# The order of input loads in a fused state-space and bilinear feed-forward kernel: three queues for one block, and both halves of the output weights in one place

## The chip, the cores and the metric

The kernel runs on one core of a Trainium2 chip. The metric is the device time of one execution in microseconds. The core has five engines that each work through their own list of instructions: PE (TensorE, matrix products), DVE (VectorE), ACT (ScalarE), POOL (GpSimd) and SP (SyncE, which here only issues transfers). Transfers between the main memory and the core's SBUF are issued from SP, ACT or POOL; each of the three has its own queue, in which requests stand in the order of the program. In the profile's list of DMA queues q1 is SP's, q10 is ACT's and q0 is POOL's.

## The reference: what is computed

Inputs are x (4 batches, 8 heads, 768 tokens, 32 values), a decay a for each token, B and C (16 values for each token), and three weight matrices. For each batch and head a state of 16 x 32 runs through the tokens; in closed form, with cum the cumulative sum of log a,

```
y[i] = sum over j <= i of (C[i] . B[j]) * exp(cum[i] - cum[j]) * x[j]
X    = y, heads side by side: 3072 tokens x 256
out  = ((X @ w_a) * (X @ w_b)) @ w_out        # 256 -> 1536 -> 256
```

The reference takes chunks of 32 tokens and carries the state from chunk to chunk; any other chunk gives the same sums.

## The kernel before

The 768 tokens are cut into six blocks of 128. A pair is two batches' share of a block, or, in the blocks after the first, four heads of all batches where B and C are concerned: pairs 0 and 1 belong to block 0, pairs 2 and 3 to block 1, pairs 4 and 5 to block 2, and so on. For each pair `scores` (line 398) multiplies C with B, `mask` (442) applies the causal mask, `outputs` (532) multiplies with x, adds the part that comes from the state and makes the sums for the next state. The feed-forward part of block k (`unit`, `bunit`: a product with w_a, a product with w_b, a copy on ACT, a multiplication on DVE; then `out_mm` or `bout` with w_out) is woven between the scores of the later blocks, so that PE always has work.

The order is written out by hand, line by line, from line 774 on: every engine takes its instructions in the order in which the program names them, and the framework adds the waits that the data need. The PSUM banks of the feed-forward part are dealt out in advance: `bank` (129) takes the next digit of the string `BANKS`, one of four banks.

What the change touches, in the order of the program:

- Loads on SP: `load_q(nc.sync, 1)` (815) loads block 1's C and B, four batches each, 64 KB a request. Then come x for pairs 2 and 3 (`load_x32`, 721; four requests of 128 KB), B for pairs 2 and 3 (`load2(nc.sync, p, 0)`, 820; `load2` makes two requests of 64 KB here), and six of the eight requests of block 2 (846). `ALL_Q` (158) lists them: C of batches 0 to 3, then B of batches 0 to 3. The last two B requests are made on POOL (904). Behind them on SP stand `loads_b(4, 5)` (847) and the later blocks' loads.
- Weights on POOL: `load_w` (182) for w_a and w_b in halves, then `load_wo(0)` (866) and `load_wo(1)` (869) for the halves of w_out, rows 0 to 5 and 6 to 11 of the tile `Wo`. The first half is used first by `out_mm(0, 0, o[0], range(6))` (907), the second by the loop of line 930.
- Decay factors: `mid_rows` (286, tile Ps), `turned_rows` (296, tile Pt, a transpose on DVE), `batch_factors` (301, tile FC, one copy for each batch, on POOL for block 1 and on ACT for the others), `batch_inverse` (308, tile FB).
- Planes: `scale_q` (341) multiplies C with FC and B with FB into a tile `planes` on POOL; `turn` (353) transposes it on DVE into `turned`, which the scores read. `scale_bc` (324) makes bm from bn, that is B by token, for the state sums (`ds_mm`, 495).
- Masks: `mask(..., by_pool=True)` copies the scores on ACT into tmp and multiplies on POOL; otherwise DVE does it.

Of the kernel before, what the change touches and what calls it, by code (L numbers as in the profile page):

```python
# [19 lines left out]
SS = 64.0  # L20

BANKS = (
    "012313213212301230123012302103120312301230132013210320132012301230132103210321023013201320"
    "1321023102310231021302130213021302130213021302310231023102310231023102310231023102310"
)


# [1 line left out]
def kernel(  # L29
# [13 lines left out]
    nc = tc.nc  # L43

    nb, H, S, D = x.shape
# [14 lines left out]
    NT = NBLK - PJ // NBP  # L60
# [79 lines left out]
    def by_token(t_):  # L140
        return t_.rearrange("p h r n -> p (h r n)").rearrange("p (t h n) -> p t h n", t=2, h=H)

    def load1(eng, p, which, bt, i0=0, n=64, to=None):
        blk, bp = divmod(p, NBP)
        if p >= P2:
            return eng.dma_start(
                by_token(pair_in[p][which])[:, bt],
                (B, C, x)[which][2 * bp + bt, :, blk * Q : (blk + 1) * Q, :].rearrange("h q n -> q h n"),
            )
        src = (B, C, x)[which][2 * bp + bt, :, blk * Q + 2 * i0 : blk * Q + 2 * i0 + 2 * n, :]  # L150
        if to is None:
            to = pair_in[p][which]
        return eng.dma_start(  # L153
            to[64 * bt + i0 : 64 * bt + i0 + n].rearrange("i h r n -> i h (r n)"),
            src.rearrange("h (i r) n -> i h (r n)", r=2),
        )

    ALL_Q = tuple((w, b) for w in (1, 0) for b in range(nb))

    def load_q(eng, blk, parts=ALL_Q):  # L160
        if blk not in by_batch:
            by_batch[blk] = [inq.tile([128, H, 4, N], f32, name=n_, tag=n_) for n_ in ("bq", "cq")]
        return [
            eng.dma_start(  # L164
                by_batch[blk][w][32 * b : 32 * b + 32].rearrange("i h s n -> i h (s n)"),
                (B, C)[w][b, :, blk * Q : (blk + 1) * Q, :].rearrange("h (i s) n -> i h (s n)", s=4),
            )
            for w, b in parts
        ]

    def load2(eng, p, which):
        if p < P2:
            return [load1(eng, p, which, bt) for bt in range(2)]
        blk, bp = divmod(p, NBP)
        src = (B, C, x)[which][2 * bp : 2 * bp + 2, :, blk * Q : (blk + 1) * Q, :]
        return [
            eng.dma_start(  # L177
                by_token(pair_in[p][which]).rearrange("p t h n -> p (t h) n"), src.rearrange("t h q n -> q (t h) n")
            )
        ]  # L180
# [6 lines left out]
    def load_wo(half):  # L187
        return nc.gpsimd.dma_start(
            Wo[:, 6 * half : 6 * half + 6].rearrange("p (g kk) e -> p g (kk e)", kk=3),
            moe_w_out.rearrange("(g p kk) e -> p g (kk e)", p=128, kk=3)[:, 2 * half : 2 * half + 2],  # L190
        )
# [94 lines left out]
    def mid_rows(lo, hi, eng):  # L286
        k = slice(lo + NBLK - NT, hi + NBLK - NT)
        eng.tensor_tensor(
            out=Ps[:, lo:hi], in0=Pr[:, k], in1=rmid[:, k].unsqueeze(2).broadcast_to((BH, hi - lo, Q)), op=ALU.mult
        )  # L290
# [10 lines left out]
    def batch_factors(lo, hi, *bs, eng=None):  # L301
        for b in bs:
            (eng.tensor_copy if eng else nc.scalar.copy)(
                FC[32 * b : 32 * b + 32, lo:hi].rearrange("p k s h -> p (k s) h"),
                Pt[:, lo:hi].rearrange("p k s (b h) -> p (k s) b h", b=nb)[:, :, b],
            )
# [91 lines left out]
    def scores(p):  # L398
        s = st[p] if p < PJ else st["U", p]
        BT, CT = s["BT"], s["CT"]  # L400
        s["T1"] = mid.tile([128, 4, 4, Q], f16, name="t1", tag="t1")

        def score(o_, b_, c_, at):
            nc.tensor.matmul(o_, b_, c_, start=True, stop=True, skip_group_check=True, tile_position=at)  # L404

        if p >= P2:
            for j, b in itertools.product(range(4), range(nb)):
                rows = slice(32 * b, 32 * b + 32)
                score(SC[b][:, j * Q : j * Q + Q], BT[rows, j], CT[rows, j // 2], (32 * b, 0))
            return  # L410
        for e, r, m, bt in itertools.product(range(2), range(2), range(4), range(2)):
            c0 = (e * 2 + r) * Q
            o_ = SC[m][64 * bt : 64 * bt + 64, c0 : c0 + Q]
            if p >= PJ:
                bp, g = divmod(m, 2)
                row = 32 * (2 * bp + bt)
                rows = slice(row, row + 32)
                b_ = BT[rows, 2 * g + e].rearrange("p (i r) -> p r i", r=2)[:, r]
                score(o_, b_, CT[rows, g], (row, 64 * bt))
            else:  # L420
                rows = slice(32 * m, 32 * m + 32)
                score(o_, BT[rows, e, r, bt], CT[rows, bt], (32 * m, 64 * bt))
# [151 lines left out]
    def state_spread(blk):  # L574
        Sbd = mid.tile([128, H // 2, 2 * D], f16, name="spair", tag="spair")
        nc.gpsimd.tensor_tensor(
            out=Sbd.rearrange("p g (e d) -> p (g e) d", e=2),
            in0=V32[:, blk].rearrange("p g (e d) -> p (g e) d", e=2),
            in1=Ge[:, blk].unsqueeze(2).broadcast_to((128, H, D)),
            op=ALU.mult,  # L580
        )
        st["S", blk + 1] = Sbd
# [10 lines left out]
    def unit_mm(p, k2, W):  # L593
        ps = bank("aps" if W is Wa else "bps")
        for kk in range(2):
            k = 2 * k2 + kk
            for f in range(2):
                nc.tensor.matmul(  # L598
                    ps[:, kk * 2 * Q : (kk + 1) * 2 * Q],
                    W[k // 6][:, f, k % 6 // 3 * 384 : (k % 6 // 3 + 1) * 384].rearrange("p (c kk) -> p kk c", kk=3)[  # L600
                        :, k % 3
                    ],
                    X2T[:, p, :, f],
                    start=(f == 0),
                    stop=(f == 1),
                    skip_group_check=True,
                )
        return ps

    def evac_a(a_ps, on_dve=False):  # L610
        asb = ffh.tile([128, 512], f32, name="asb", tag="asb")
        (nc.vector.tensor_copy if on_dve else nc.scalar.copy)(asb, a_ps)  # L612
        return asb

    def times(p, k2, b_ps, asb, by_pool=False):
        s = st[p]
        if "hk" not in s:
            s["hk"] = ffh.tile([128, NK, 2 * Q], f16, name="hk", tag="hk")
        eng = nc.vector
        if by_pool:  # L620
            eng, b_ps = nc.gpsimd, evac_a(b_ps)
        eng.tensor_tensor(  # L622
            out=s["hk"][:, 2 * k2 : 2 * k2 + 2, :].rearrange("p k q -> p (k q)"), in0=b_ps, in1=asb, op=ALU.mult
        )

    def unit(p, k2, between=None, by_pool=False):
        a_ps = unit_mm(p, k2, Wa)
        if between:
            between()
        b_ps = unit_mm(p, k2, Wb)  # L630
        asb = evac_a(a_ps)
        return lambda: times(p, k2, b_ps, asb, by_pool)
# [78 lines left out]
    def loads_b(*ps):  # L711
        for p in ps:
            if p < NP:
                tiles(p)
                load2(nc.sync, p, 0)
# [30 lines left out]
    def spread(blk):  # L746
        if blk < NBLK - 1:
            state_spread(blk)
            state_decay(blk)
# [67 lines left out]
    for p in (2, 3):  # L817
        tiles(p)
    x_in = [load_x32(p) for p in (2, 3)]
    for p in (2, 3):  # L820
        load2(nc.sync, p, 0)
    warmup(tcp, 512, 512)
    transposes(1, apart=True)
    aps = [unit_mm(0, 0, Wa)]
# [18 lines left out]
    for m in range(3):  # L843
        mask(product(1, m))
    bps = [unit_mm(0, k2, Wb) for k2 in range(3)]
    load_q(nc.sync, 2, ALL_Q[:6])
    loads_b(4, 5)
    times(0, 0, bps[0], asb[0])
    times(0, 1, bps[1], asb[1], by_pool=True)
# [13 lines left out]
    nc.vector.reciprocal(flat(fB, 1, 2), fps[:, 2 * NBP * H : 4 * NBP * H])  # L863
    times(0, 2, bps[2], asb[2])
    turned_rows(0, 1)
    load_wo(0)
    batch_factors(0, 1, *range(nb), eng=nc.gpsimd)
    mid_rows(1, NT, nc.gpsimd)
    load_wo(1)
    go((1, 0))  # L870
    batch_inverse(0, 1)
# [12 lines left out]
        op=ALU.mult,  # L884
    )
    spread(0)
    late = ((0, 3), (0, 4), (1, 3))
    aps = [unit_mm(p, k2, Wa) for p, k2 in late]
    asb = [evac_a(a_ps) for a_ps in aps]
    batch_factors(2, NT, *range(nb))  # L890
    for (p, k2), a_sb_ in zip(late, asb):
        times(p, k2, unit_mm(p, k2, Wb), a_sb_)
        if k2 == 4:
            turn(2)
    go((0, 5))
    h = unit(1, 4)
    scores(2)
    turn(3)
    mask(product(2, 3), by_pool=True)
# [1 line left out]
    h()  # L901
    h5 = unit(1, 5)
    mask(product(2, 2), by_pool=True)
    load_q(nc.gpsimd, 2, ALL_Q[6:])
    mask(product(2, 1))
    o = [bank("ops"), bank("ops")]
    out_mm(0, 0, o[0], range(6))
    out_mm(0, 1, o[1], range(6))
    batch_factors(1, 2, 0, 1)
    h5()  # L910
    o.append(bank("ops"))
    out_mm(1, 0, o[2], range(6))
    scores(3)
    mask(product(3, 3), by_pool=True)
    batch_factors(1, 2, 2, 3)
    scale_bc(2, 0, nc.gpsimd)
    scale_bc(3, 0, nc.gpsimd)
    nc.gpsimd.memset(causal_q, SS)
# [11 lines left out]
    for c in range(3):  # L930
        p, bt = divmod(c, NBP)
# [136 lines left out]
```

## Time and profile before

| what | us |
|---|---|
| median of 3 runs | 122.37 (122.28 to 123.07) |
| the profiled execution | 122.9 |
| its span, first to last instruction | 121.2 |
| PE busy in it | 115.9 |
| DVE, ACT, POOL busy | 90.2, 67.4, 58.7 |

The profile shows one execution. A timeline line gives the start, the duration, the engine, the line of the kernel and the operation with what it writes and reads, then, in brackets, the idle time of the engine ahead of it and what ended it. Lines that say "x4" merge instructions that follow each other. An issue of a transfer has a duration of its own, the time that it held the issuing queue; from the issue to the landing of the data is a time of its own again, and is given in the list of issues. The granted clock of PE was 1.00 in every stretch that is looked at here. A list of DMA queues gives packets, megabytes and the time of the packets as a share of 16 engines; it can exceed 100% where packets overlap.

### The profile page before, as it was taken

The numbers are of one execution on the slowest core, as the hardware profiler recorded it, in microseconds if no ns is written. First come the engines' busy times: TensorE is split into PE (matmuls) and PEld (weight loads), VectorE is DVE, ScalarE is ACT, GpSimd is POOL, SyncE is SP. The second block draws the span as 40 slices with busy tenths as digits, with TensorE's granted clock in tenths as the row PEclk, the third lists the DMA queues.
The fourth block names the chain that finished last, engine by engine and source line by source line (L and its number), as shares of the span: only waits on it lengthen the run. The fifth ranks groups of instructions, "written<-read, shape, count | busy, mean of one in ns | idle before, by whom it ended". The sixth has DMA issues, their size and how long they took to land.

```text
span 121.2 us, 3577 instructions
## 1 busy us (share of the span) xinstructions
PE 115.9 (96%) x1399; PEld 75.5 (62%) x1400; DVE 90.2 (74%) x165; ACT 67.4 (56%) x135; POOL 58.7 (48%) x92
## 2 busy tenths in 40 slices
PE   7989999999999999999999999999999999999990
PEld 5646799788644478644475464775465684645880
DVE  4998889799989995599966999677899426748000
ACT  0446659648567655577566737635735637475230
POOL 7994887997479999386902994200000000000000
PEclk9999999999999999999999999999999999999999
DMA  2999999986769996999992919012001111010131
GB/s 62 135 172 194 205 216 187 206 123 135 113 90 102 145 112 119 102 108 145 200 239 89 86 5 124 7 46 92 0 0 46 44 43 48 0 43 0 49 121 52
DMA packets 59297, 12.13 MB, mean 100 GB/s; under 512 B 54480, under 2 KB 59216, under 8 KB 59280
## 3 DMA queue, kind: packets, MB, share of 16 engines
q0 software_dynamic: 20320, 3.80, 38.3%
q1 hardware_dynamic: 36432, 7.74, 33.8%
q10 hardware_dynamic: 2528, 0.36, 1.8%
q8 instruction: 11, 0.18, 0.7%
q14 instruction: 6, 0.05, 0.1%
HBM read 12.42 MB, written 3.15 MB: 128 GB/s over the span
## 4 chain that ended last, share of the span: by engine, by line
PE 68%; DMA 14%; SPq 10%; POOL 3%; issue 1%; DVE 0%; ACT 0%; POOLq 0%
PE ops L693 22%; PE aps L667 20%; PE bps L667 20%; SPq L153 8%; DMA cq<-in_C_dram 6%; DMA Wa<-in_moe_w_a_dram 5%; DMA bq<-in_B_dram 3%; PE SC L404 2%; SPq L164 2%; PE SC L473 2%; POOL xn L153 1%; PE SC L536 1%; POOL causal L225 1%; POOL planes L346 1%; DVE turned L359 0%
## 5 line engine op out<-in xcount | busy, mean ns | idle before, releaser
L612 ACT COPY asb<-aps 128x512 f32<-128x512 f32 x72 | 41.9, 586 | 15.6 <-PE aps L667 13.3
L679 DVE TENSOR_TENSOR hkb<-bps,asb 128x512 f16<-128x512 f32 x60 | 40.3, 687 | 11.9 <-ACT asb L612 10.5
L667 PE MATMUL aps<-XB,Wa 128*128 128x512 f16 x120 | 35.8, 379 | 0.0
L667 PE MATMUL bps<-XB,Wb 128*128 128x512 f16 x120 | 35.7, 379 | 0.0
L693 PE MATMUL ops<-Wo,hkb 128*128 128x256 f16 (+1 forms) x252 | 28.1, 268 | 0.0
L693 PEld LDWEIGHTS <-hkb 128*128 128x128 f16 x252 | 23.0, 98 | 3.8
L667 PEld LDWEIGHTS <-Wb 128*128 128x128 f16 x120 | 12.4, 103 | 13.5
L667 PEld LDWEIGHTS <-Wa 128*128 128x128 f16 x120 | 12.1, 103 | 11.5 <-issue 0.2
L449 DVE TENSOR_TENSOR t<-SC,causal_q 128x512 f16<-128x512 f32 x27 | 17.3, 682 | 2.4 <-PE SC L404 2.4
L705 ACT ACTIVATE osb<-ops 128x256 f32<-128x256 f32 (+1 forms) x20 | 7.6, 378 | 18.4 <-PE ops L693 18.4
L447 POOL TENSOR_TENSOR t<-tmp,causal_q 128x512 f16<-128x512 f32 x5 | 5.8, 1157 | 8.8 <-ACT tmp L446 8.8
L177 POOL DMA_DIRECT2D xn<-in_x_dram x8 | 9.5, 1190 | 0.0
L346 POOL TENSOR_TENSOR planes<-bq,FB 128x256 f16<-128x256 f32 x10 | 7.5, 770 | 2.0 <-DMA bq<-in_B_dram 1.4
L446 ACT COPY tmp<-SC 128x512 f32<-128x512 f32 x10 | 5.9, 588 | 4.1 <-PE SC L404 3.8
L346 POOL TENSOR_TENSOR planes<-cq,FC 128x256 f16<-128x256 f32 x10 | 7.6, 775 | 0.9 <-DMA cq<-in_C_dram 0.8
L449 DVE TENSOR_TENSOR t<-SC,causal 128x512 f16<-128x512 f32 x11 | 7.0, 681 | 0.7 <-PE SC L404 0.6
L622 DVE TENSOR_TENSOR hk<-bps,asb 128x512 f16<-128x512 f32 x11 | 7.2, 670 | 0.2 <-ACT asb L612 0.2
L598 PE MATMUL aps<-X2T,Wa 128*128 128x256 f16 x48 | 6.8, 274 | 0.0
L558 ACT ACTIVATE XB<-SC 128x512 f16<-128x512 f32 (+1 forms) x9 | 4.6, 548 | 4.1 <-PE SC L501 2.4
L598 PE MATMUL bps<-X2T,Wb 128*128 128x256 f16 x48 | 6.6, 273 | 0.1
L359 DVE STREAM_TRANSPOSE turned<-planes 128x384 f32<-128x384 f32 x10 | 5.5, 564 | 1.1 <-POOL planes L346 1.1
L447 POOL TENSOR_TENSOR t<-tmp,causal 128x512 f16<-128x512 f32 x5 | 5.7, 1154 | 0.3
(101 smaller groups left out, 110.6 us busy)
## 6 DMA issues: line engine op xcount, KB each, us to landing
out_dram<-osb SPq DMA_DIRECT2D x23, 128.0 KB, 1.9
cq<-in_C_dram SPq DMA_DIRECT2D x20, 64.0 KB, 2.7
bq<-in_B_dram SPq DMA_DIRECT2D x18, 64.0 KB, 3.8
bn<-in_B_dram SPq DMA_DIRECT2D x8, 128.0 KB, 3.9
xn<-in_x_dram POOLq DMA_DIRECT2D x8, 128.0 KB, 5.2
Wa<-in_moe_w_a_dram POOLq DMA_DIRECT2D x2, 384.0 KB, 7.4
Wb<-in_moe_w_b_dram POOLq DMA_DIRECT2D x2, 384.0 KB, 8.0
Wo<-in_moe_w_out_dram POOLq DMA_DIRECT2D x2, 384.0 KB, 6.8
```

The source lines that it names most:

```text
L153: return eng.dma_start(to[64 * bt + i0 : 64 * bt + i0 + n].rearrange("i h r n -> i h (r n)"), src.rearrange("h (i r) n -> i h (r n)", r=2),)
L177: eng.dma_start(by_token(pair_in[p][which]).rearrange("p t h n -> p (t h) n"), src.rearrange("t h q n -> q (t h) n"))
L346: eng.tensor_tensor(out=plane[:, c0 : c0 + 4 * step].rearrange("p (j c) s -> p j s c", c=step)[:, :, :, 0:N], in0=by_batch[blk][which][:, ...
L447: nc.gpsimd.tensor_tensor(out=o_, in0=tmp, in1=c_, op=ALU.mult)
L449: nc.vector.tensor_tensor(out=o_, in0=i_, in1=c_, op=ALU.mult)
L598: nc.tensor.matmul(ps[:, kk * 2 * Q : (kk + 1) * 2 * Q], W[k // 6][:, f, k % 6 // 3 * 384 : (k % 6 // 3 + 1) * 384].rearrange("p (c kk) -> ...
L612: (nc.vector.tensor_copy if on_dve else nc.scalar.copy)(asb, a_ps)
L622: eng.tensor_tensor(out=s["hk"][:, 2 * k2 : 2 * k2 + 2, :].rearrange("p k q -> p (k q)"), in0=b_ps, in1=asb, op=ALU.mult)
L667: nc.tensor.matmul(t_, W[k // 6][:, f, k % 6 // 3 * 384 : (k % 6 // 3 + 1) * 384].rearrange("p (c kk) -> p kk c", kk=3)[:, k % 3], XB[:, b ...
L679: return lambda: nc.vector.tensor_tensor(out=s["hk"][:, k], in0=ps[1], in1=asb, op=ALU.mult)
L693: nc.tensor.matmul(o_ps[:, 0:w], hk[:, k, c * Q : (c + 1) * Q], Wo[:, k, cs], start=(k == 0), stop=(k == NK - 1), skip_group_check=True,)
L705: nc.scalar.activation(out=o_sb[:, 0:w], in_=o_ps[:, 0:w], func=AF.Copy, scale=1.0 / (YS * YS))
```

## The change

Four loads change their queue or their place, six copies of factors change their place on ACT, and the string of banks is replaced.

- The two requests for pair 3's B go from SP to POOL, behind `spread(0)`.
- Of block 2's eight requests SP makes five (C of batch 3, B of batches 0 to 3), and ACT makes the first three (C of batches 0 to 2), at the place where POOL made two.
- `load_wo(0)` goes from ahead of `batch_factors(0, 1, ...)` on POOL to behind `mid_rows(1, NT, ...)`, directly ahead of `load_wo(1)`.
- The factors of block 2 (`batch_factors(1, 2, ...)`) are copied earlier: batch 0 together with those of the later blocks, batches 1 to 3 behind unit (1, 4).

```
@@ BANKS: from the 28th digit on another string
-    for p in (2, 3):
-        load2(nc.sync, p, 0)
+    load2(nc.sync, 2, 0)
...
-    load_q(nc.sync, 2, ALL_Q[:6])
+    load_q(nc.sync, 2, ALL_Q[3:])
...
     turned_rows(0, 1)
-    load_wo(0)
     batch_factors(0, 1, *range(nb), eng=nc.gpsimd)
     mid_rows(1, NT, nc.gpsimd)
+    load_wo(0)
     load_wo(1)
...
     spread(0)
+    load2(nc.gpsimd, 3, 0)
     late = ((0, 3), (0, 4), (1, 3))
     aps = [unit_mm(p, k2, Wa) for p, k2 in late]
     asb = [evac_a(a_ps) for a_ps in aps]
-    batch_factors(2, NT, *range(nb))
+    batch_factors(1, NT, 0)
+    batch_factors(2, NT, 1, 2, 3)
...
     h = unit(1, 4)
+    batch_factors(1, 2, 1, 2, 3)
     scores(2)
...
     mask(product(2, 2), by_pool=True)
-    load_q(nc.gpsimd, 2, ALL_Q[6:])
+    load_q(nc.scalar, 2, ALL_Q[:3])
     mask(product(2, 1))
...
     out_mm(0, 1, o[1], range(6))
-    batch_factors(1, 2, 0, 1)
     h5()
...
     mask(product(3, 3), by_pool=True)
-    batch_factors(1, 2, 2, 3)
```

More of the change, by code (lines that the diff above doesn't have):

```diff
@@ L22 @@
 BANKS = (
-    "012313213212301230123012302103120312301230132013210320132012301230132103210321023013201320"
-    "1321023102310231021302130213021302130213021302310231023102310231023102310231023102310"
+    "012313213212301230123012302013021302310231032103201321032102310231032013201320123103210321"
+    "0320123012301230120312031203120312031203120312301230123012301230123012301230123012301"
 )
@@ L819 @@
     x_in = [load_x32(p) for p in (2, 3)]
-    for p in (2, 3):
-        load2(nc.sync, p, 0)
+    load2(nc.sync, 2, 0)
     warmup(tcp, 512, 512)
@@ L845 @@
     bps = [unit_mm(0, k2, Wb) for k2 in range(3)]
-    load_q(nc.sync, 2, ALL_Q[:6])
+    load_q(nc.sync, 2, ALL_Q[3:])
     loads_b(4, 5)
@@ L865 @@
     turned_rows(0, 1)
-    load_wo(0)
     batch_factors(0, 1, *range(nb), eng=nc.gpsimd)
     mid_rows(1, NT, nc.gpsimd)
+    load_wo(0)
     load_wo(1)
@@ L886 @@
     spread(0)
+    load2(nc.gpsimd, 3, 0)
     late = ((0, 3), (0, 4), (1, 3))
@@ L889 @@
     asb = [evac_a(a_ps) for a_ps in aps]
-    batch_factors(2, NT, *range(nb))
+    batch_factors(1, NT, 0)
+    batch_factors(2, NT, 1, 2, 3)
     for (p, k2), a_sb_ in zip(late, asb):
@@ L896 @@
     h = unit(1, 4)
+    batch_factors(1, 2, 1, 2, 3)
     scores(2)
@@ L903 @@
     mask(product(2, 2), by_pool=True)
-    load_q(nc.gpsimd, 2, ALL_Q[6:])
+    load_q(nc.scalar, 2, ALL_Q[:3])
     mask(product(2, 1))
@@ L908 @@
     out_mm(0, 1, o[1], range(6))
-    batch_factors(1, 2, 0, 1)
     h5()
@@ L914 @@
     mask(product(3, 3), by_pool=True)
-    batch_factors(1, 2, 2, 3)
     scale_bc(2, 0, nc.gpsimd)
```

## The prediction

> **What bounds the kernel now.** I read the busy table first, then the waits of PE, then PE's timeline around the change, then the timelines of the queues that the change touches.
>
> ```profile
> PE 115.9 (96%) x1399; PEld 75.5 (62%) x1400; DVE 90.2 (74%) x165; ACT 67.4 (56%) x135; POOL 58.7 (48%) x92
> ```
>
> PE is occupied for 115.9 of 121.2 us. Its waits hold only one item that belongs to data arriving late after the first 10 us:
>
> ```profile
> PE SC L404 <- DVE turned L359: 0.4, 2, 0.2
> ```
>
> Two score groups wait for a turned plane, 0.4 us together. The timeline places them, and places the first use of the output weights:
>
> ```profile
> 22.57 0.65 PE L404 MATMUL SC<-turned 32*64 32x128 f16 x32 [0.16 <-DVE turned L359]
> ...
> 24.05 2.17 PE L637 MATMUL ops<-Wo,hk 128*128 128x256 f16 x18
> ...
> 35.42 0.40 PE L404 MATMUL SC<-turned 32*128 32x128 f16 x16 [0.24 <-DVE turned L359]
> ```
>
> So in this region a better order of loads can win 0.4 us at most, and the matmuls at 24.05 must not be made to wait. PE's order of work is not touched: after 35.42 it never idles, and what is added or taken ahead of that arrives at the end in full.
>
> The second wait starts in SP's queue. The chain of work that ended last shows it (start, duration):
>
> ```profile
> 29.97 3.85 DMA bq<-in_B_dram
> 33.98 0.78 POOL planes L346
> 34.78 0.59 DVE turned L359
> ```
>
> and SP's and ACT's timelines show why that load is issued so late and where ACT has room:
>
> ```profile
> 17.63 3.85 SPq L153 DMA_DIRECT2D x<-in_x_dram  x4
> 21.52 5.75 SPq L153 DMA_DIRECT2D bn<-in_B_dram  x4
> 27.32 2.11 SPq L164 DMA_DIRECT2D cq<-in_C_dram  x4
> 29.48 0.94 SPq L164 DMA_DIRECT2D bq<-in_B_dram  x2
> ```
> ```profile
> 24.29 0.59 ACT L446 COPY tmp<-SC 128x512 f32<-128x512 f32 x1
> 24.77 0.44 ACT L303 COPY FC<-Pt 32x32 f32<-32x32 f32 x2
> 26.88 0.58 ACT L446 COPY tmp<-SC 128x512 f32<-128x512 f32 x1 [1.67 <-PE SC L404]
> ```
>
> POOL's timeline holds the requests of the output weights and the chain to the first wait:
>
> ```profile
> 15.39 0.75 POOL L188 DMA_DIRECT2D Wo<-in_moe_w_out_dram  x1
> 16.39 0.93 POOL L303 COPY FC<-Pt 32x32 f32<-32x32 f32 x4 [0.25 <-DVE Pt L297]
> 17.40 1.03 POOL L288 TENSOR_TENSOR Ps<-Pr,rmid 32x512 f32<-32x512 f32 x1
> 18.39 0.75 POOL L188 DMA_DIRECT2D Wo<-in_moe_w_out_dram  x1
> 19.16 1.38 POOL L346 TENSOR_TENSOR planes<-cq,FC 128x256 f16<-128x256 f32 x2
> 21.14 1.37 POOL L346 TENSOR_TENSOR planes<-bq,FB 128x256 f16<-128x256 f32 x2 [0.60 <-DVE hk L622]
> ```
>
> **Part 1, the first half of Wo requested behind the middle rows.** Its 0.75 us go from 15.39. Nothing starts earlier for it: the FC copies behind it wait 0.25 us for Pt, whose transpose on DVE ends at 15.93 + 0.39 = 16.32. So FC and Ps stay at 16.39 and 17.40, the first half is requested at 18.4 (3.0 later), the second at 19.1 (0.75 later), and the planes of pairs 2 and 3 start at 19.9. The two C planes (1.38) then end at 21.3. The B planes start now at 21.14, behind a wait that I put down to the load of bq: its last request, at 14.67, lands 6.3 later by the issue list, at 20.97. At 21.3 that wait is gone and they start 0.14 later. Turned plane and scores follow: **+0.14** on PE, the 0.16 becoming 0.30.
>
> **Part 2, whether that half lands in time.** PE needs it at 24.05 + 0.14 = 24.2. The trace has no such request into an empty queue, so I bound it. Now the first half is issued at 15.39 and lands in 7.0 us, at 22.4; the second lands at 18.39 + 6.5 = 24.9, so one half behind another takes 2.5 us. From 16.9 to 17.7 us POOL's queue moved almost nothing:
>
> ```profile
> q1 hardware_dynamic: 638, 0.15, 135.2%
> q0 software_dynamic: 4, 0.00, 2.2%
> ```
>
> so the first half began only some 2.3 us after its request and took 4.7. Low end: a POOL load of 64 KB at 26.19 (bq) lands in 2.5 us; the other five sixths of a half at the 2.5 us rate make 2.1, together 4.6: landing at 23.0, no wait. Upper ends: its own 7.0, landing at 25.4, wait 1.2; and the Wa and Wb rows, 7.4 and 8.0 us in the median, 8.5 at most: waits of 1.6 to 2.7. I take a start after 2.3 as now and 3.8 for the transfer, between 2.5 and 4.7 but nearer to the latter, since SP's queue still carries the x, B and block 2 loads beside it: 6.1, landing at 24.5. **+0.3**. All that follows on PE shifts by this; no other engine loses, since all have slack. The second half, some 2.5 later at 27.0, is needed at 30.90.
>
> **Part 3, pair 3's B on POOL.** Two issues (0.6 each, by the bq row on POOL at 26.19: 1.22 for two) come at 24.0, ahead of the two masks of 23.97 to 26.2, which end 1.2 later at 27.4; the 1.22 of bq loads goes away behind them, so the mask at 27.54, which waits for ACT's copy (26.88 + 0.58), stays. PE reads these masks from 29.70: 2.3 us of cover, cost 0. The loads stand behind both halves of Wo: 27.0 + 2.5 = 29.5 at the latest row. The product that needs them (bm, 0.62) starts at 29.89 now, after a 0.61 wait for the same load, and PE reads it from about 30.6. Cost 0, and up to 0.5 if they land a microsecond later.
>
> **Part 4, SP and ACT.** SP's third and fourth bn loads begin at 24.80 and 25.47 and last 0.63 and 1.80. Without them block 2's five loads start at 24.8 instead of 27.3 and end at about 27.2 (0.47 each). With the slowest landing there, 3.9, the last is in at 30.6 instead of 33.8. ACT issues three C loads from 24.9. Its own issues at the start took 0.61 to 0.70 each, SP's of this kind 0.45 to 0.63: 1.35 to 2.1 us in a gap that is 2.0 wide once its two FC copies are gone. Behind them stands the copy at 26.88 for a mask that PE reads after 29.70: cost 0; an issue that stalls as SP's did (2.34 is the longest there) has about one microsecond of cover. The three FC copies (0.66) fall into ACT's idle 0.73 ahead of 23.31: 0. So POOL's waits of 0.81 for cq and 1.38 for bq (31.82 and 33.98) go, and the planes of pair 4 are done by about 32.5. What is late next is DVE's order: the turn stands behind the product of 33.73 + 0.69, runs from 34.42 to 35.0, and the scores start when PE is free, at 35.18. **-0.24**.
>
> **Part 5, the banks.** From the 28th place on the string is the old one with 0 and 1 exchanged; only the two banks of unit (1, 5) trade reuse distances (5 and 3 become 2 and 6). Its first bank is then free when ACT has copied aps (22.57), its second when DVE has read bps at about 23.2, ahead of 23.6. 0.
>
> **Sum**: 0.14 + 0.3 - 0.24 = +0.2. The profiled execution took 122.9 us around its span of 121.2; the median of the three runs is 122.37. The difference goes on the median: **122.6 us**. One per cent, 1.2 us, is about what a measurement of this kernel can tell from no change.
>
> The Trainium skill speaks against the sharing. The row first: from 21 to 24 us the DMA engines' share is 1.13 at 205 GB/s, from 27 to 30 it is 0.60 at 125 GB/s. The page "DMA: Bandwidth & Descriptors", section "Issuing engines are not separate DMA queues", says that DMAs from several engines run on the same 16 DMA engines and that only issue time is saved. Where the engines are full that would leave the 0.24 us where it is and the sum at +0.44; at 27 to 30 the row shows room, so I keep the gain.
>
> **Rivals.**
>
> *The weights come late* (slower). The half lands 7.0 us or more after its request, because SP's earlier loads crowd the same time. For it: its own row, and Wa and Wb. Against: those stood behind other weights or behind a backlog. With 7.0 the wait is 1.2 and the sum +1.1: 123.5. It passes 1% from a landing of 7.1 us on; with 8.0 it is 124.5. Chance 0.30, most of it (0.25) above 1%.
>
> *The weights are in time.* The half lands by 24.2. For it: the queue is empty, and 4.6 us is the low bound. Sum 0.14 - 0.24 = -0.1: 122.3, down to 122.0 if the 0.14 also goes. Chance 0.18. The Trainium skill's page "DMA: Bandwidth & Descriptors", section "Anatomy of one DMA", has a fit for transfers issued from GpSimd, 2.0 us plus bytes over 436 GB/s, which gives an estimate of 2.9 us for 384 KB, a landing at 21.3 and so this case's sum; no row here is near it (6.5 and 7.0, with other transfers ahead).
>
> *The loads don't land earlier.* The backlog that Wo adds from 20 to 27 us stalls SP's issues, and bq lands at 33.8 as now. For it: the 2.34 us issue, made while Wo was moving. Sum 0.14 + 0.3 = +0.44 and, with pair 3's B late, up to +0.9: 122.8 to 123.3. Chance 0.10.
>
> **Numbers.** Forecast (0 to +0.6, its own range 122.4 to 123.0) 0.36, late weights 0.30, in time 0.18, no earlier loads 0.10, something that no row shows 0.06, half of it a gain and half a loss above 1%. So slower by over 1%: 0.25 + 0.03 = 0.28; faster: 0.03; within: 0.69. The range from 121.9 to 124.2 leaves out landings of over 7.7 us and unseen gains.
>
> **What would show it.** In the changed profile: Wo's two requests at 18.4 and 19.1; an idle time ahead of PE's L637 group near 24.2, named after the Wo load, 0.3 by the forecast, 1.2 by the first rival; scores near 22.7 with 0.30 idle; none ahead of the scores near 35.4; SP's last bq issue near 27. An ACT issue above 1.5 us, or a wait of PE for a bank, would make the working wrong.

## The result, and the profile after

The changed kernel takes 124.04 us (median of 5 runs, 123.68 to 124.24), the kernel before beside it 122.49 (122.28 to 123.07): ratio 1.0123, 95% interval 1.0095 to 1.0151. Run once more later it gave 123.67 us and 1.0115 (1.0087 to 1.0142). So the change costs 1.2%, some 1.5 us. That is inside the range that was given, but beyond the 1% that its likeliest case stayed within. The profiled execution took 123.68 us, the fastest of the five, around a span of 122.0, while the profile of before is of one that took 122.9, above its median. So the two profiles differ by only 0.8 us. PE is as busy as before, in a longer span:

```profile
PE 115.8 (95%) x1399; PEld 75.3 (62%) x1400; DVE 90.3 (74%) x165; ACT 67.3 (55%) x134; POOL 58.9 (48%) x92
```

PE's waits of the changed kernel (who waits for whom, us in total, times, longest):

```profile
PE ds L512 <- POOL bm L333: 1.0, 2, 0.9
```

The wait for the turned planes that the change could remove is gone from this list. In its place stands one that the kernel before didn't have: the products for the state sums (`ds_mm`) wait for bm. The timelines place it. PE's in the kernel before, where the L512 products are mixed with the end of L485's:

```profile
29.70 0.77 PE L485 MATMUL SC<-t,xn 64*32 64x128 f16 x61
...
30.31 0.65 PE L512 MATMUL ds<-xn,bm 64*32 64x64 f16 x29
30.90 0.83 PE L637 MATMUL ops<-Wo,hk 128*128 128x256 f16 x6
```

PE's in the changed kernel:

```profile
29.41 0.81 PE L485 MATMUL SC<-t,xn 64*32 64x128 f16 x64
31.08 0.41 PE L512 MATMUL ds<-xn,bm 64*32 64x64 f16 x16 [0.86 <-POOL bm L333]
31.66 0.41 PE L512 MATMUL ds<-xn,bm 64*32 64x64 f16 x16 [0.17 <-POOL bm L333]
32.00 0.83 PE L637 MATMUL ops<-Wo,hk 128*128 128x256 f16 x6
...
36.21 0.40 PE L404 MATMUL SC<-turned 32*128 32x128 f16 x16
```

Before, L485 began at 29.70 and the next L637 group at 30.90: 1.20 us. Now that stretch takes 2.59, **1.39 more** (in a second profile of the changed kernel, experiment 11, it takes 1.91, 0.71 more). The scores at 36.21 have no idle time ahead of them: from 32.00 to there it is 4.21 us, against 4.52 before, **0.31 less**. And this execution reached L485 0.29 earlier. Together +0.79, the difference of the spans. The 0.29 can't be put down to the change: in the second profile of the changed kernel L485 begins at 29.78. Most of that difference arises far ahead of the loads that were moved. PE's second group of transposes (L374) waits for a B load that is requested on ACT near 3.6 us, and begins half a microsecond after it lands, at 10.12 us in the first profile of the changed kernel, at 10.47 in the second, and at up to 11.42 in the experiments' profiles. One profile is therefore compared stretch by stretch here, not by its whole time.

bm waits for B, as POOL's timeline shows:

```profile
18.15 1.46 POOL L188 DMA_DIRECT2D Wo<-in_moe_w_out_dram  x2
...
23.50 1.43 POOL L153 DMA_DIRECT2D bn<-in_B_dram  x2
...
27.65 1.16 POOL L447 TENSOR_TENSOR t<-tmp,causal 128x512 f16<-128x512 f32 x1 [0.44 <-ACT tmp L446]
30.41 1.20 POOL L333 TENSOR_TENSOR bm<-bn,fB 128x256 f16<-128x256 f32 x2 [1.60 <-DMA bn<-in_B_dram]
```

POOL was ready at 28.8 and got B 1.6 us later. It isn't only pair 3's B, which went to POOL. The chain that ended last names pair 2's, still on SP and requested at much the same time as before (21.05 and 21.75 against 21.52 and 22.41):

```profile
21.75 8.53 DMA bn<-in_B_dram
30.41 0.45 POOL bm L333
```

It took 8.5 us to land, at 30.27; before, 5.7 us, at 28.09. SP's timeline of the changed kernel has the same backlog: its first C request (22.92) stalls for 2.82 us, and the four B requests of block 2, which were to be made early, stretch until 30.6:

```profile
17.46 3.54 SPq L153 DMA_DIRECT2D x<-in_x_dram  x4
21.05 1.83 SPq L153 DMA_DIRECT2D bn<-in_B_dram  x2
22.92 2.82 SPq L164 DMA_DIRECT2D cq<-in_C_dram  x1
25.78 4.82 SPq L164 DMA_DIRECT2D bq<-in_B_dram  x4
```

What stood ahead of these loads, the stretches tell. Columns: stretch, its length, PE busy (matmuls), granted clock, share of the DMA engines, GB/s. The kernel before:

```profile
17.50:20.50 3.00, 3.00 (x30) 1.00 1.29 204
20.50:23.50 3.00, 2.84 (x53) 1.00 1.10 190
23.50:26.50 3.00, 3.00 (x49) 1.00 1.09 164
26.50:29.50 3.00, 3.00 (x54) 1.00 0.58 115
```

The changed kernel:

```profile
17.50:20.50 3.00, 3.00 (x30) 1.00 0.68 98
20.50:23.50 3.00, 2.99 (x55) 1.00 1.06 185
23.50:26.50 3.00, 3.00 (x55) 1.00 1.20 223
26.50:29.50 3.00, 3.00 (x53) 1.00 1.31 177
```

From 17.5 to 20.5 us the DMA engines now move 98 GB/s in place of 204: the first half of w_out isn't requested yet, and SP has only x to offer. That is 0.32 MB missing, some 1.6 us of work at 200 GB/s, and it is made up between 23.5 and 29.5, just where x and B of pairs 2 and 3 have to land. In the second profile the stretch has 136 GB/s, so there some 0.2 MB or 1.0 us are missing.

### The profile page after: what moved, and what is told of

The parts are those of the page before. It is cut to its first block, busy times and chain, and to the rows that moved or that the text cites. A ratio compares the mean times of both kernels' runs of the same rounds, so it can differ in the third digit from the quotient of the medians.

```text
span 122.0 us, 3573 instructions
## 1 busy us (share of the span) xinstructions
PE 115.8 (95%) x1399; PEld 75.3 (62%) x1400; DVE 90.3 (74%) x165; ACT 67.3 (55%) x134; POOL 58.9 (48%) x92
## 4 chain that ended last, share of the span: by engine, by line
PE 71%; DMA 18%; POOL 3%; SPq 3%; issue 1%; ACT 0%; POOLq 0%
PE ops L693 22%; PE aps L667 22%; PE bps L667 21%; DMA bn<-in_B_dram 7%; DMA cq<-in_C_dram 6%; DMA Wa<-in_moe_w_a_dram 5%; SPq L153 3%; PE SC L404 2%; PE SC L473 2%; POOL xn L153 1%; POOL bm L333 1%; PE SC L536 1%; POOL causal L225 1%; PE ops L637 1%; PE SC L501 0%
```

## The experiments

The first guess was theory A: the late weights push the B loads back. Its rival B: the three queues do it, by running ACT's C and POOL's B beside pair 2's B. All ratios are to the kernel before, timed on the same chip in the same round.

**1. The changed kernel, the first half of w_out early again.**

```
+    load_wo(0)
     batch_factors(0, 1, *range(nb), eng=nc.gpsimd)
     mid_rows(1, NT, nc.gpsimd)
-    load_wo(0)
     load_wo(1)
```

> The changed kernel with the request of the first half of the output weights put back ahead of the FC copies; the loads stay on three queues. Theory A (the late weights fill 20 to 26 us, and SP's x and B loads land behind them): pair 2's B lands by about 28.2 as before, POOL's wait for it falls from 1.60 us to under 0.3, PE's wait at the state sums (1.2 us) goes, and the wait of 0.24 before the scores near 35.4 stays away: about 122.2 us, 0.2 below before. Theory B (ACT's C loads and POOL's B loads run at the same time as pair 2's B and hold it up, whenever the weights come): pair 2's B still lands at 29.5 or later, PE's wait stays at 0.8 us or more, 123.3 us or more.

122.34 us, ratio 0.9995 (0.9969 to 1.0020). POOL's timeline and the first stretch of this kernel:

```profile
28.41 0.62 POOL L333 TENSOR_TENSOR bm<-bn,fB 128x256 f16<-128x256 f32 x1
29.52 0.62 POOL L333 TENSOR_TENSOR bm<-bn,fB 128x256 f16<-128x256 f32 x1 [0.49 <-DMA bn<-in_B_dram]
```
```profile
17.50:20.50 3.00, 3.00 (x29) 1.00 1.27 203
```

The DMA engines are full again from 17.5 on, pair 2's B lands at 27.9, and PE waits neither for bm nor for the turned planes. The whole loss goes with this one line. But sharing the loads among three queues brings nothing that these runs can measure either, though the planes of pair 4 are no longer late. (The interval reaches from 0.38 us faster to 0.24 slower, so the gain of 0.24 that was forecast for it isn't excluded.)

**2. The kernel before, with only that request moved.**

```
-    load_wo(0)
     batch_factors(0, 1, *range(nb), eng=nc.gpsimd)
     mid_rows(1, NT, nc.gpsimd)
+    load_wo(0)
     load_wo(1)
```

> The kernel before, with only the first half of the output weights requested behind the middle rows; all loads on their old queues. Theory A: pair 2's B lands at 29 or later and pair 3's, behind it on SP, at 30 or later; PE waits 1 us or more at the state sums: 123.3 us or more. Theory B: pair 2's B lands by 28.3, no such wait, 122.4 to 122.7 us.

123.31 us, 1.0065 (1.0040 to 1.0091). Pair 2's B lands at 29.75, pair 3's at 30.14, the first stretch moves 116 GB/s. The direction is A's, and B's 122.7 is excluded. But it is half of the loss: the other half needs the shared queues as well. And PE's list has only 0.2 us for bm, where A had expected 1 us or more.

**3 and 4. The changed kernel with one of the two shared loads back on SP.** In the third all of block 2's loads, in the fourth pair 3's B:

```
-    load_q(nc.sync, 2, ALL_Q[3:])
+    load_q(nc.sync, 2)
...
-    load_q(nc.scalar, 2, ALL_Q[:3])
```
```
-    load2(nc.sync, 2, 0)
+    for p in (2, 3):
+        load2(nc.sync, p, 0)
...
-    load2(nc.gpsimd, 3, 0)
```

> The changed kernel with all eight loads of block 2 on SP, none on ACT; the weights late, pair 3's B on POOL. Theory A: no better than the changed kernel, 123.7 to 124.2 us, pair 2's B at 29 or later. Theory B: pair 2's B lands by 28.5, because nothing but POOL's B stands beside it, and most of the 1.5 us comes back: 122.7 us or less.

> The changed kernel with pair 3's B back on SP behind pair 2's; the weights late, three C loads of block 2 on ACT. Theory A: pair 2's B at 29 or later, pair 3's later still, 123.5 us or more. Theory B with POOL's loads as the cause: pair 2's B by 28.5, 122.9 us or less.

123.25 us, 1.0069 (1.0042 to 1.0096), and 123.46 us, 1.0062 (1.0034 to 1.0090). Both lie between the expectations. Either step takes back about half, to what the late request alone costs in the second experiment. In both, pair 2's B lands at 28.0, and pair 3's at 30.2 and 29.5. So by the times the late request costs half of the loss without any sharing, and with late weights the two shared loads together add the rest. The landings alone would speak for B, but the fourth's profile is of its fastest run, 0.9 below its median. Nor do the profiles show the whole 0.8 us that each of experiments 2 to 4 loses: from L485 to the next L637 group PE takes 1.49, 1.34 and 1.31 us, against 1.20 in the kernel before and 1.1 where nothing waits. Where the rest arises stays open.

**5. The changed kernel, bm made from data that landed long ago.**

```
-        raw = by_token(pair_in[p][which]) if p >= P2 else pair_in[p][which].rearrange(...)
+        src = pair_in[p - PJ][1] if PJ <= p < P2 else pair_in[p][which]
+        raw = by_token(src) if p >= P2 else src.rearrange(...)
```

> The changed kernel, but the products bm of pairs 2 and 3 read C of pairs 0 and 1, which has long landed, in place of B of pairs 2 and 3; all loads are still made. So block 1's part of the state sums isn't computed from its own B. Theory A (late weights push the B of pairs 2 and 3 behind the point where the state sums need it, and that wait is the whole cost): PE's wait at the state sums is gone, 122.2 to 122.6 us. Rival C (the cost lies in several waits that differ from execution to execution, such as PE's wait for the first half of the weights): 123.2 us or more.

122.65 us, 1.0021 (0.9996 to 1.0046). All transfers are still made, only nothing waits for these B any more (so the state sums of block 1 aren't those of the reference), and some 1.0 of the 1.2% are gone. PE's wait for bm is therefore most of the cost. PE's waits, in the slowest of the twelve runs, show what may be left:

```profile
PE ops L638 <- DMA Wo<-in_moe_w_out_dram: 0.7, 1, 0.7
```

That is the wait that the prediction had looked for; here the half landed at 25.3, 6.4 us after its request.

**6 and 8. Both halves of w_out together, but early**, in the changed kernel (6) and in the kernel before (8):

```
+    load_wo(0)
+    load_wo(1)
     batch_factors(0, 1, *range(nb), eng=nc.gpsimd)
     mid_rows(1, NT, nc.gpsimd)
```

> The changed kernel with both halves of the output weights requested together, but early, ahead of the FC copies. Theory A (what costs is that they come late): both halves land by 24.5, B of pairs 2 and 3 by 29, no wait for bm on PE, 122.0 to 122.5 us; the FC copies start some 0.5 us later, which the planes take back because no request stands ahead of them any more. Rival (what costs is that they come together): B at 30 or later, 123.2 us or more.

> The kernel before with both halves of the output weights requested early, ahead of the FC copies. Theory A: the B loads land no later than before (28.3 and 29.8), the planes of pairs 2 and 3 start a quarter of a microsecond earlier, the wait of 0.24 near 35.4 stays: 122.1 to 122.5 us, no measurable difference. If the second half early crowds the loads of block 1 and x: 122.8 us or more.

122.76 us, 1.0013 (0.9992 to 1.0034), and 122.78 us, 1.0007 (0.9981 to 1.0033). It isn't that the halves come together, but that they come late. No wait for bm shows in either profile. What is new there is a small one near 19 us, 0.3, because the factors are copied later.

**7. The changed kernel, B of pairs 2 and 3 ahead of x on SP.**

```
+    for p in (2, 3):
+        load2(nc.sync, p, 0)
     x_in = [load_x32(p) for p in (2, 3)]
-    load2(nc.sync, 2, 0)
...
-    load2(nc.gpsimd, 3, 0)
```

> The changed kernel with B of pairs 2 and 3 requested on SP ahead of the x loads of pairs 2 and 3; the weights late, three C loads on ACT. Theory A: B of pair 3 lands by 26.5 and nothing waits for bm; x lands about 1.3 us later than in the changed kernel, near 28.5, and ACT's cast of it may hold PE up by 0 to 0.5 us: 122.3 to 123.0 us. If instead the one slow DMA engine at 26.6 to 31 is the cause by itself, whatever is queued, x or the C loads take the delay and PE waits 1 us or more elsewhere: 123.3 us or more.

124.54 us, 1.0154 (1.0126 to 1.0183): a miss, no faster than the changed kernel. B was there by 25.8. But x, four times 128 KB, came later by far more than the 1.3 us expected, the last at 31.1 in place of 27.3. ACT's casts of it, from ACT's timeline:

```profile
29.27 0.62 ACT L725 CAST xn<-x 128x512 f16<-128x512 f32 x1 [0.31 <-DMA x<-in_x_dram]
31.22 0.62 ACT L725 CAST xn<-x 128x512 f16<-128x512 f32 x1 [1.33 <-DMA x<-in_x_dram]
```

PE's products L485, which read the cast, stood for 0.46 us until the second one was done (PE's list names an instruction of POOL that ended at the same time; in the changed kernel these products ran ahead of that one). So a wait went from B to x, the load that now stood last. But this profile doesn't show that the order of the loads made the whole loss: PE also waited 0.4 for the weights, and the early wait at L374 took 1.2, ahead of everything that the edit moves. The first stretch moved only 90 GB/s and the next 119; in this late execution the weights were requested at 19.5, 1.3 later than in the changed kernel's profile. This made theory D out of A: what counts is how much the DMA engines moved before 20.5 us, and the loads at the end of the line pay for what they didn't.

**9. The changed kernel, the first half between the FC copies and the middle rows.**

```
     batch_factors(0, 1, *range(nb), eng=nc.gpsimd)
+    load_wo(0)
     mid_rows(1, NT, nc.gpsimd)
-    load_wo(0)
     load_wo(1)
```

> The changed kernel with the first half of the output weights requested one place earlier, between the FC copies and the middle rows, about 1.1 us earlier than in the changed kernel and 1.9 later than before; the second half as in the changed kernel. Theory D (the late request leaves the DMA engines half idle from 17.5 to 20.5 us, 98 against 204 GB/s, and the 0.3 MB that is missing there is made up for ahead of the B loads): 130 to 170 GB/s in that stretch, the B loads about half a microsecond earlier than in the changed kernel, 122.8 to 123.6 us. Rival E (the cost depends on the second half or on its place behind the first, not on when the first starts): as the changed kernel, 123.7 us or more.

123.64 us, 1.0112 (1.0071 to 1.0153), between the two expectations and no better than the changed kernel beside it (123.67). The first stretch moved 136 GB/s, as much as in the changed kernel's second profile, and pair 2's B landed at 29.1. Inconclusive as a test of dose: the request came earlier, and the hole didn't shrink. The runs together don't bear out D's measure either. Where the time is that of before and the weights are early, the first stretch moves 201 GB/s or more; with late weights it moves 90 to 145, but there it doesn't put the losses in order: 116 to 124 GB/s (experiments 2 to 4) go with 0.6 to 0.7%, 136 (9 and 11) with 1.1%.

**10. The changed kernel without the second half of w_out.** The output products of rows 6 to 11 read rows 0 to 5.

```
     load_wo(0)
-    load_wo(1)
...
-                    Wo[:, k, :]
+                    Wo[:, k % 6, :]
...
```

> The changed kernel without the load of the second half of the output weights; the second half of the output products reads the first half in its place. So the output isn't that of the reference, and 384 KB in SBUF less are loaded ahead of the B loads; the first half is requested as late as in the changed kernel. Theory D: the stretch of 17.5 to 20.5 us stays half idle, but the traffic that B stands behind is gone, B lands 1.5 us or more earlier, no wait for bm: 122.0 to 122.7 us. If B's lateness isn't a matter of the traffic ahead of it (one slow DMA engine, SP's issue times): 123.2 us or more.

122.41 us, 1.0012 (0.9985 to 1.0038). The first stretch is as empty as ever, and the first half was requested at 18.7, but with less traffic behind it B lands at 26.8 and 27.6 (pair 2) and 28.0 and 29.5 (pair 3), and bm runs without a wait:

```profile
17.50:20.50 3.00, 3.00 (x30) 1.00 0.58 107
20.50:23.50 3.00, 3.00 (x56) 1.00 0.94 159
```
```profile
29.51 1.20 POOL L333 TENSOR_TENSOR bm<-bn,fB 128x256 f16<-128x256 f32 x2
```

So it is the traffic that the late request leaves ahead of B that makes the wait for bm. This profile, of the second slowest of twelve runs, also shows that a late request can cost something of its own: the first half landed at 24.88, and the output products that read it began at 24.93, 2.26 us after PE's scores in place of 1.47 in the changed kernel. (PE's list puts this down to an instruction of DVE that ended at the same time; in the changed kernel the products ran ahead of that one.)

**11. The changed kernel once more.**

> The changed kernel once more, beside the two others on the same chip: 123.5 to 124.3 us, with the waits of PE split between the first half of the weights (0 to 0.8 us) and bm (0.3 to 1.5 us) in another proportion than in its first profile.

123.67 us, 1.0115 (1.0087 to 1.0142). PE waits 0.6 for bm in this profile and not for the weights, which landed at 24.1.

**12. The changed kernel, pair 3's B requested on POOL behind the last w_b request**, where POOL was idle:

```
     load_w(1, Wb)
+    for p in (2, 3):
+        tiles(p)
+    load2(nc.gpsimd, 3, 0)
...
     spread(0)
-    load2(nc.gpsimd, 3, 0)
```

> The changed kernel with pair 3's two B requests on POOL moved early, directly behind the last request for w_b, where POOL is idle for 1.5 us; the weights as late as in the changed kernel. Theory D (the DMA engines' empty time from 17.5 to 20.5 us is what is lost): the 128 KB are moved in or ahead of that stretch, pair 3's B lands by 20, pair 2's about 0.6 us earlier than in the changed kernel, PE's wait for bm falls below 0.4 us: 122.3 to 123.0 us with the weights still late. If late weights cost by something else than B standing behind them: 123.5 us or more.

123.45 us, 1.0065 (1.0039 to 1.0091): half of the loss comes back, less than expected. Pair 3's B landed at 18.9, and the first stretch moved 145 GB/s, against 98 and 136 in the changed kernel's two profiles. But x began 0.6 later and pair 2's B landed at 30.1 in this profile, hardly earlier than in the changed kernel. By its time, filling part of the hole helps, and by less than was expected; the profile doesn't show it, since from L485 to the next L637 group PE takes 2.07 us, no less than in the changed kernel's second profile; why pair 2's second request stayed so late isn't settled. No version here beats the kernel before; the first experiment equals it.

## Why the prediction was right and wrong, by its own steps

**The bound was read rightly.** From the scores near 36 us to the end all 14 profiles take 85.6 to 85.8 us, so what happened ahead of them arrived at the end. The range held, and the sign was the forecast's, but that was luck: the size was 1.5 us against 0.2, the range was wide for the sake of another transfer, and the mechanism was none of its cases.

**Part 1 (+0.14).** The wait at these scores is in the list of neither profile of the changed kernel; by the starts of its matmuls PE loses 0.18 and 0.27 there, 0.33 before. The term is too small to be told from what differs between executions. "Nothing starts earlier for it" held: the FC copies waited for Pt before and after. What the sum left out is that block 1's B loads, with no weights beside them, had landed by 19.4 and 19.6 in place of 20.9, so the B planes no longer waited.

**Part 2 (+0.3).** The half landed 5.5 and 5.6 us after its request in the two profiles of the changed kernel, not 6.1, and PE didn't wait. In other profiles with late weights it did: PE's list has 0.7 and 0.4 for it in the fifth and seventh experiments, and in the fourth and tenth the first of these products began 0.05 us after the landing, 0.25 and 0.8 us later after PE's scores than in the changed kernel. So the size was fair on average, but it isn't what the changed kernel's profiles lose.

**Part 3 (cost 0) is the step that failed.** It priced POOL's B, with "up to 0.5", and never asked when pair 2's B lands on SP. Measured: pair 2's at 30.3 and 29.3, pair 3's at 30.8 and 30.6, and 1.39 us more on PE in the first profile, 0.71 in the second. The tables that could have shown it were read: the prediction used the 0.8 us in which POOL's queue moved almost nothing to time the weights, and said that SP's queue "still carries the x, B and block 2 loads beside it". It counted this against the weights alone. The sum to make was of bytes: 384 KB asked for three microseconds later, through engines that were full (204, then 190 GB/s) until 23.5. Such a sum gives 1.0 to 1.6 us of work to be made up. It doesn't explain why the queues' sharing doubles the loss; that stays open.

**Part 4 (-0.24).** Came out: 0.31 less on PE ahead of these scores. But SP's five loads weren't issued by 27.2; the last was issued at 30.29 and landed at 33.2. The planes of pair 4 were done at 34.2 and not at 32.5, in time for a PE that was itself later. In the first experiment, without that delay, the scores find their plane ready too (the last B load at 31.2), and the time still doesn't move measurably. ACT's third request had to stand for some 2 us, beyond the one microsecond of cover that this part gave; the copy behind it began about 0.4 later after its scores than before, and PE lost nothing by it.

**Part 5 (banks, 0).** No wait of PE for a bank is in the lists.

**The rivals.** "The weights come late" had about the right price and the right sign, from the same edit, but for the wrong transfer and at the wrong place. "The loads don't land earlier" named the backlog and the stalls of SP's issues, with the row to prove it, and priced only their effect on block 2's loads and pair 3's B, 0.9 at most.

## What to carry to other kernels

In this kernel, with DMA engines that were full, a request that was moved later took its place from the loads behind it, on another queue too. In such a case add up the bytes that are no longer moved in the time given up, divide by the measured rate, and look for the load with the least slack at the end of the line; the moved transfer itself may be in time. Here a request made early enough kept the DMA engines busy and saved 1.2%; spreading requests over three queues saved nothing measurable.

## What the runs showed of the hardware that was not expected

**While the weights pass, the queues share by packets, not by bytes.** In the changed kernel from 21.0 to 22.5 us (packets, MB, share of 16 engines):

```profile
q0 software_dynamic: 157, 0.24, 90.7%
q1 hardware_dynamic: 156, 0.04, 20.1%
```

The numbers of packets are equal, and POOL's queue, with 1.5 KB a packet, moves six times the bytes of SP's, with 256 B. So the weight transfer on POOL took 0.24 of the 0.28 MB moved, though x and B stood on SP. The Trainium skill, "DMA: Bandwidth & Descriptors", section "Queues, rings and completion order", says that each DMA engine goes round the queues that it has work for, packet by packet; the trace agrees (157 to 156). Its section "Issuing engines are not separate DMA queues" says that requests from several engines run on the same 16 DMA engines; this case's time doesn't speak against it: with the weights early, three queues gave a ratio of 0.9995 (0.9969 to 1.0020).

**ACT waited for SP's load.** ACT's timeline of the changed kernel, at its third C request:

```profile
26.63 0.32 ACTq L164 DMA_DIRECT2D cq<-in_C_dram  x1
26.99 0.58 ACT L446 COPY tmp<-SC 128x512 f32<-128x512 f32 x1 [2.27 <-DMA x<-in_x_dram]
```

The requests of SP and ACT take the same eight semaphores in turn, so this one had to wait until SP's third x load had landed, at 26.61. Three of SP's B requests likewise start within 0.03 us of the landing of the request eight places ahead (27.25, 29.29, 30.27). A request that is spread to another engine can hold that engine up; here it put ACT's next copy off by about 0.4 us.

**The last share decides.** A load lands in 16 shares, and bm waits for the last. Of pair 2's second B request 14 shares had landed by 27.97 in the changed kernel, the others at 28.99 and 30.27; before, 14 by 27.03 and the last at 28.09. So in this profile only 0.9 of the 2.2 us is common to the 14 shares, and the last two add 1.2. In the second profile nearly all of it is common: 14 by 28.34, the last at 29.26. An instruction load of 16 KB ran on one DMA engine from 26.63 for 1.43 us. That it held up the late shares, with three queues waiting behind it on that engine, would explain why sharing doubles the loss; no run separates it, and it stays open. One thing speaks for looking there: this instruction load begins at 24.2 to 25.3 us in the five profiles of the kernel before and of experiments 1, 6, 8 and 10, which lose nothing measurable, and at 26.0 to 27.8 in all others (the fifth, where nothing waits for B, among them). Whether it comes later because the engines are busier, or adds to the loss by itself, isn't known.
